# Linear attention, Fourier mixing and MLP on one core: attention of two batches in turns, and two plain MLP groups instead of four

## The chip, the cores and the metric

The kernel runs on one core of a Trainium2 chip. The metric is the device time of one execution in microseconds (us), a median over several runs. The run-to-run spread of one kernel is about 1%.

## The reference

Four batches of 768 rows go through a decaying linear attention with 8 heads of 64, and the result x (768 x 512 a batch) through a Fourier mixing block with an MLP:

```python
# attention, per block of 64 rows (cut)
intra = einsum('bhic,bhjc->bhij', qb, kb) * Dmask
out   = einsum('bhij,bhjd->bhid', intra, vb) + einsum('bhid,bhde->bhie', qb * lam_pow, kv_state)
kv_state = lam_block * kv_state + einsum('bhsd,bhse->bhde', kb * rev_pow, vb)

# mixing and MLP
X = fft(fft(x, axis=1), axis=2)
u = x + real(X)
un = (u - mean(u)) / sqrt(var(u) + 1e-06)
return u + maximum(un @ w_ch1, 0.0) @ w_ch2      # w_ch1 512 x 2048, w_ch2 2048 x 512
```

The two weights arrive with 64-bit elements and are decoded on the chip.

## The kernel before

All is fp32. A batch's attention has six chunks of 128 rows. Its transform folds x with its mirror image on VectorE, multiplies by tables on TensorE (`ys`), and then for three pairs of row tiles (t = 1, 2, 0) multiplies again, adds x, normalises and transposes into `ut`, the input of an MLP group. A group is two tiles of 128 rows; there are twelve. **Plain** groups are multiplied as they stand, from SBUF, while the front (attention, transforms) still runs. **Late** groups wait in device memory for the end, where two of them are done at a time with seven products instead of eight, which needs sums of weight blocks.

```python
    xp = plain_pool("xp", 2 * NC - 2)          # x tiles
    hp_ = plain_pool("hp", FO // 4 + 1)        # raw 64-bit weights, and hidden rows of plain groups
    pa = psums.enter_context(tc.tile_pool(name="pa", bufs=5, space=PS))
    pm = psums.enter_context(tc.tile_pool(name="pm", bufs=3, space=PS))
    # ... cut
    ORDER = [(b, g) for b in range(B) for g in (1, 2, 0)]
    PLAIN, LATE = ORDER[:4], ORDER[4:]
    # ... cut: the order, as generators whose pieces are woven
    run(weave(attn(0), part(w, 0.5 * NW), 0.5 * NW / t_att))
    fr, mix = chain(front(b) for b in range(1, B)), fft_ln(0)     # front = attention, then transform
    # ... cut: transform 0 woven with attention 1 and weights
    back = chain(mlp(b, g) for b, g in PLAIN)
    run(weave(part(fr, 2 * t_chunk), weave(part(back, FO * 1.7 - 1.0), w, 0.9), 1.5))
    run(w)
    run(weave(fr, back, (len(PLAIN) * t_mlp - FO * 1.7 - 25.0) / t_rest))
    # ... cut
    run(weave(combine_weights(0), back, 1.5))
    # ... cut
    run(combine_weights(1))
    for j in range(len(LATE) // 2):
        late(j)
```

A scheduler then orders each engine's instructions, mostly as the program has them, by what it takes to be ready and by free buffers. The program then fixes that order for each engine.

## Time and profile before

| kernel before | |
|---|---|
| time | 912.4 us (904.8 to 912.7) |
| span in the trace | 906.4 us, mean granted TensorE clock 0.975 of full speed |
| first late pair | at 513.1 us; four pairs of 96.7 us follow |
| TensorE busy ahead of it | 439.4 us, idle 73.6 us |

"Ahead of it" is what the change reorders: the rest is late pairs and some 7 us of end. The prediction shows the lines.

### The profile page before, as it was taken

Reading aid. Unit: us, or ns where it says so; the run is one execution under the profiler, and the core shown is the slowest. Engines: PE = TensorE matmul, PEld = TensorE weight load, DVE = VectorE, ACT = ScalarE, POOL = GpSimd, SP = SyncE. Lnnn points to the kernel's source line nnn. Section 1 sums busy time; section 2 is a strip of 40 time slices with the busy share of each in tenths; the row PEclk is TensorE's granted clock in tenths of the full one; section 3 lists DMA queues with packets and bytes.
Section 4 is the critical chain, followed back from the end, with each engine's and each line's share of the span. In section 5 each row is a group of like instructions: output and inputs, shape, how many; then the busy total and the mean of one; then the engine's idle time right before and its main releaser. Section 6 shows DMA issues by size and latency. Waiting matters only on the chain.

```text
span 906.4 us, 11761 instructions
## 1 busy us (share of the span) xinstructions
PE 826.5 (91%) x4660; PEld 652.9 (72%) x4660; DVE 437.0 (48%) x1006; ACT 209.0 (23%) x467; POOL 90.7 (10%) x108
## 2 busy tenths in 40 slices
PE   4775678699999999999999899999999999999997
PEld 2564566545865578567874588888888888888886
DVE  4779869854532135443567756115531454135410
ACT  3665436620211212223221021002200120012100
POOL 2214211100010110012200100000000000000000
PEclk9988789899999999999999999999999999999999
DMA  9899316611013241344216001110011100110010
GB/s 230 232 249 252 111 52 179 209 39 35 24 47 93 74 120 47 116 141 129 88 47 215 29 1 47 46 35 12 1 59 47 35 1 1 47 47 1 0 35 24
DMA packets 96190, 72.43 MB, mean 80 GB/s; under 512 B 77536, under 2 KB 79080, under 8 KB 96136
## 3 DMA queue, kind: packets, MB, share of 16 engines
q1 hardware_dynamic: 90176, 57.51, 22.3%
q0 software_dynamic: 2496, 7.87, 2.7%
q10 hardware_dynamic: 3464, 6.30, 2.0%
q8 instruction: 37, 0.61, 0.3%
q14 instruction: 17, 0.14, 0.0%
HBM read 50.68 MB, written 20.99 MB: 79 GB/s over the span
## 4 chain that ended last, share of the span: by engine, by line
PE 51%; DVE 5%; issue 1%; DMA 1%; POOL 1%; ACT 0%; POOLq 0%; DVEq 0%; ACTq 0%
PE p L627 21%; PE p L674 21%; PE pm L545 1%; PE pm L559 1%; PE pa L440 1%; PE pa L486 1%; PE pa L290 1%; PE pa L322 1%; DVE stt L470 1%; DVE w1s L604 1%; DVE w2s L604 1%; PE pa L318 1%; POOL rs L475 0%; DVE x L512 0%; DVE x L513 0%
## 5 line engine op out<-in xcount | busy, mean ns | idle before, releaser
L545 PE MATMUL pm<-ut,w 128*128 128x256 f32 x512 | 124.2, 392 | 10.0 <-ACT hr L553 8.2
L559 PE MATMUL pm<-w,hr 128*128 128x512 f32 x256 | 120.6, 602 | 0.0
L545 PEld LDWEIGHTS pm<-ut,w 128*128 128x128 f32 x512 | 95.9, 194 | 26.3 <-ACT hr L553 8.9
L627 PE MATMUL p<-ur,w 128*128 128x256 f32 x384 | 95.1, 382 | 3.3 <-DVE ur L620 1.9
L627 PEld LDWEIGHTS p<-ur,w 128*128 128x128 f32 x384 | 73.3, 191 | 14.5 <-issue 2.3
L559 PEld LDWEIGHTS pm<-w,hr 128*128 128x128 f32 x256 | 44.8, 190 | 40.3 <-issue 38.8
L627 PE MATMUL p<-us,w1s 128*128 128x256 f32 x256 | 66.6, 383 | 0.0
L674 PE MATMUL p<-w,hs 128*128 128x256 f32 x256 | 58.0, 379 | 0.5 <-DVE y L695 0.5
L674 PE MATMUL p<-w2s,hs 128*128 128x256 f32 x256 | 57.9, 379 | 0.0
L674 PE MATMUL p<-w,ha 128*128 128x256 f32 x256 | 57.9, 379 | 0.0
L535 POOL DMA_INDIRECT out_dram<-y,ix x12 | 13.3, 1109 | 409.9 <-DVE y L698 370.9
L627 PEld LDWEIGHTS p<-us,w1s 128*128 128x128 f32 x256 | 49.2, 192 | 6.9
L674 PEld LDWEIGHTS p<-w,hs 128*128 128x128 f32 x256 | 48.5, 190 | 7.5 <-DVE y L695 0.9
L674 PEld LDWEIGHTS p<-w2s,hs 128*128 128x128 f32 x256 | 48.6, 190 | 6.6
L674 PEld LDWEIGHTS p<-w,ha 128*128 128x128 f32 x256 | 48.6, 190 | 6.6
L290 PEld LDWEIGHTS pa<-qT,kT 64*128 64x128 f32 x384 | 30.1, 193 | 25.9 <-ACT qT L279 14.4
L654 ACT COPY ha<-p 128x256 f32<-128x256 f32 x32 | 11.9, 372 | 155.6 <-PE p L627 155.5
L290 PE MATMUL pa<-qT,kT 64*128 64x128 f32 x384 | 36.2, 291 | 11.7 <-ACT qT L279 10.0
L294 DVE TENSOR_TENSOR sc<-pa,decay 128x512 f32<-128x512 f32 x48 | 31.8, 684 | 29.1 <-PE pa L290 26.3
L322 PE MATMUL pa<-sc,v 128*64 128x128 f32 x384 | 31.2, 290 | 9.8 <-DVE sc L294 9.8
L665 DVE TENSOR_TENSOR ha<-p,ha 128x256 f32<-128x256 f32 x32 | 13.6, 425 | 47.1 <-ACT ha L664 47.1
L322 PEld LDWEIGHTS pa<-sc,v 128*64 128x64 f32 x384 | 23.4, 143 | 17.5 <-DVE sc L294 13.4
(141 smaller groups left out, 1188.3 us busy)
## 6 DMA issues: line engine op xcount, KB each, us to landing
raw<-in_moe_w_ch_dram SPq DMA_DIRECT2D x32, 512.0 KB, 5.2
k<-in_k_dram SPq DMA_DIRECT2D x24, 256.0 KB, 3.8
q<-in_q_dram SPq DMA_DIRECT2D x24, 256.0 KB, 3.9
v<-in_v_dram SPq DMA_DIRECT2D x24, 256.0 KB, 3.2
ud<-x SPq DMA_DIRECT2D x16, 256.0 KB, 2.1
utd<-ut SPq DMA_DIRECT2D x8, 512.0 KB, 3.3
u<-ud SPq DMA_DIRECT2D x16, 256.0 KB, 2.6
ur<-utd SPq DMA_DIRECT2D x8, 512.0 KB, 5.6
```

Source lines behind the costliest of these rows:

```text
L290: mm(pss[hi][:, hp, :], lhsT=kT[HD[hi], hp, :], rhs=qT[HD[hi], hp, :], start=True, stop=True)
L294: nc.vector.tensor_tensor(t, pss[hi], decay[:, hi::2, :], op=ALU.mult)
L318: mm(po[HD[hi], hp, :], lhsT=s_old[HD[hi], hp, :], rhs=qs[HD[hi], hp, :], start=(hp == 0), stop=False, skip_group_check=True)
L322: mm(po[HD[hi], hp, :], lhsT=vt[:, 2 * hp + hi, :], rhs=sc[hi][:, hp, :], start=(c == 0 and hp == 0), stop=(hp == HP - 1), skip_group_chec ...
L535: nc.gpsimd.indirect_dma_start(out=out.rearrange("b s d -> (b s) d"), out_offset=row_of(2 + HC * (b + 1) + T - HC), in_=y[:, :], in_offset ...
L545: nc.tensor.matmul(ps, lhsT=w1[:, c, 128 * fc:128 * fc + 128], rhs=ut[:, c, :], start=(c == 0), stop=(c == KO - 1))
L559: nc.tensor.matmul(ps, lhsT=hr[fc // 4][:, fc % 4, 128 * i:128 * i + 128], rhs=w2[:, fc, :], start=(fc == 0), stop=(fc == FO - 1))
L604: V.tensor_tensor(o[:, i:i + n // 2], x[:, i:i + n // 2], y[:, i:i + n // 2], op=op)
L627: nc.tensor.matmul(ps, lhsT=s2.A[a][:, kt, 128 * i:128 * i + 128], rhs=U[b][:, kt, :], start=(first and kt == 0), stop=(kt == 1), skip_gro ...
L654: nc.scalar.copy(a11, two(X))
L665: V.tensor_tensor(a22, two(Z), a22, op=ADD)
L674: nc.tensor.matmul(ps, lhsT=h[a][:, s, i, :], rhs=s2.B[b][:, i, :], start=(first and i == 0), stop=(i == HF - 1), skip_group_check=True)
```

## The change

The intent: a late pair costs TensorE less than a plain pair, so two of the four plain groups become late. The filler that they were is to be replaced by the attention of two batches in turns. To make room in SBUF, x goes through device memory and comes back when a transform wants it, one x tile and one buffer of `hp` are given up, and work moves from VectorE to ScalarE and GpSimd. The core of the diff (cut: indices of the mirror rows, the two sets of states, the fetches of x):

```diff
-    xp = plain_pool("xp", 2 * NC - 2)
+    xp = plain_pool("xp", 2 * NC - 3)
-    hp_ = plain_pool("hp", FO // 4 + 1)
+    hp_ = plain_pool("hp", FO // 4)
-    pa = ... bufs=5     pm = ... bufs=3
+    pa = ... bufs=6     pm = ... bufs=2
-            qs = new(at, [128, HP, C], "qs")
+            qs = new(at, [128, HP, C], "qs", bufs=2)
+            nb = new(np_, [128, G], "nb")
+            nc.vector.scalar_tensor_tensor(nb, mv[:, :, 0], -1.0, rs, op0=ALU.mult, op1=ALU.mult)
-                    nc.vector.tensor_scalar(o, x, mv[:, i, 0:1], rs[:, i:i + 1], op0=ALU.subtract, op1=ALU.mult)
+                    nc.scalar.activation(o, x, AF.Identity, bias=nb[:, i:i + 1], scale=rs[:, i:i + 1])
-    PLAIN, LATE = ORDER[:4], ORDER[4:]
+    PLAIN, LATE = ORDER[:2], ORDER[2:]
-            if fc % 2: nc.vector.tensor_scalar(t, ps, 0.0, None, op0=ALU.max)
-            else:      nc.scalar.activation(t, ps, AF.Relu)
+            nc.scalar.activation(t, ps, AF.Relu)
+            eng = nc.gpsimd if part == 0 and n >= 3 else V        # combining: half on GpSimd
+    att = chain([turns([attn(0), attn(1)]), turns([attn(2), attn(3)])])
+    mix = [fft_ln(b) for b in range(B)]
+    back, back2 = (mlp(b, g) for b, g in PLAIN)
+    run(weave(part(att, 2 * t_att - 1.0), part(w, 0.6 * NW), 0.6 * NW / (2 * t_att)))
+    # cut: transform 0 with 4 chunks of attention 2 and 3 and the rest of the weights;
+    #      transform 1 with 3 chunks and back; the last chunks with back;
+    #      transforms 2 and 3 with back2, a few us between their steps and 0.3 of their pace within
```

More of the change, by code (lines that the diff above doesn't have):

```diff
@@ L59, in _consts @@
     p = np.arange(128)
-    ha, hb = S - 256, 128 * (S // 256) + 128
+    hb = S - 256
     rev = [S - 128 * t - p for t in range(S // 256)]
-    rows = [S // 2 - 128 - p, np.maximum(S // 2 - 256 - p, 0)]
-    rows += [r - hb for r in rev[:2]] + [r - 128 for r in rev[2:]]
+    rows = [S // 2 - p, S // 2 - 128 - p]
+    rows += [r - hb for r in rev[:2]] + rev[2:]
     for b in range(B):
@@ L132 @@
     psums = ctx.enter_context(ExitStack())
-    pa = psums.enter_context(tc.tile_pool(name="pa", bufs=5, space=PS))
-    pm = psums.enter_context(tc.tile_pool(name="pm", bufs=3, space=PS))
+    pa = psums.enter_context(tc.tile_pool(name="pa", bufs=6, space=PS))
+    pm = psums.enter_context(tc.tile_pool(name="pm", bufs=2, space=PS))
     cnt = [0]
@@ L193 @@
     nc.gpsimd.memset(mhalf, -0.5)
-    st = [const.tile([128, HP, D], F32, name=f"st{i}") for i in range(2)]
+    st = [[const.tile([128, HP, D], F32, name=f"st{j}{i}") for i in range(2)] for j in range(2)]
     cs = const.tile([128, 2, 2, 2, NK], F32, name="cs")
@@ L249, in weights @@
             yield 1.0
-    xs, xn_, xd = {}, {}, {}
+    xs, xd = {}, {}
     def pair(t, hp):
@@ L296, in attn_chunk @@
         yield 1.5
-        s_old, s_new = st[(c + 1) % 2], st[c % 2]
+        s_old, s_new = st[b % 2][(c + 1) % 2], st[b % 2][c % 2]
         if not last:
@@ L330, in attn_chunk @@
         px = px.rearrange("p h e -> p (h e)")
-        x = xn_[b, c] = new(xp, [C, DM], "x") if c < HC else new(xn, [C, DM], "xn")
+        x = new(xn, [C, DM], "xn")
         nc.scalar.copy(x[:, 0:HM], px[:, 0:HM])
@@ L334, in attn_chunk @@
         if c == 0:
-            xd[b] = (dram.tile([S - 256, DM], F32, name=f"xa{b}"), dram.tile([257, DM], F32, name=f"xb{b}"))
+            xd[b] = (dram.tile([S - 128, DM], F32, name=f"xa{b}"), dram.tile([257, DM], F32, name=f"xb{b}"))
             nc.scalar.dma_start(xd[b][1][256:257], x[0:1])
-        elif c < NC - 1:
-            nc.scalar.dma_start(xd[b][0][(c - 1) * C:c * C], x)
+        if c < NC - 1:
+            nc.scalar.dma_start(xd[b][0][rows], x)
         if c >= NC - 2:
             nc.scalar.dma_start(xd[b][1][(c - NC + 2) * C:(c - NC + 3) * C], x)
-        if c == NC - 2:
-            mirror_a(b)
-        elif c == NC - 1:
-            mirror_b(b)
+        if b == 0 and c == NC - 2:
+            fetch_a(b)
         yield 1.7
@@ L357 @@
     gather = nc.gpsimd.indirect_dma_start
-    eo, r1s = {}, {}
+    eo, r1s, x3s = {}, {}, {}
     def fold_x(b, a, n, i, lo, hi):
@@ L368, in fold_x, with fetch_a @@
         tt(o[0:n, i, 1:HM], o[0:n, i, 1:HM], o[0:n, i, HM:DM - 1], op=ALU.subtract)
-    def mirror_a(b):
+    def fetch_a(b):
         xa = xd[b][0]
@@ L377, in mirror_a @@
             gather(out=r1[a][0:n], out_offset=None, in_=xa[:, :], in_offset=row_of(a, n))
+            nc.sync.dma_start(eo[b][a][1][0:n, 1, 0:DM], xa[S // 2 + 128 * a:S // 2 + 128 * a + n])
         for t in range(2, HC):
@@ L380, in mirror_a, with fetch_b @@
             gather(out=u[:, :], out_offset=None, in_=xa[:, :], in_offset=row_of(2 + t))
-    def mirror_b(b):
+        for t in range(HC):
+            u = xs[b, t] = new(xp, [128, DM], "x")
+            nc.sync.dma_start(u, xa[128 * t:128 * t + 128])
+    def fetch_b(b):
         for t in range(2):
@@ L385, in mirror_b @@
             gather(out=u[:, :], out_offset=None, in_=xd[b][1][:, :], in_offset=row_of(2 + t))
-        for t in range(HC):
-            xs[b, t] = xn_.pop((b, t))
     def fold_a(b):
@@ L391, in fold_a @@
         for a, n in enumerate(BLK):
-            fold_x(b, a, n, 1, r1[a][0:n], xn_[b, HC + a][0:n])
+            fold_x(b, a, n, 1, r1[a][0:n], eo[b][a][1][0:n, 1, 0:DM])
+        x3s[b] = new(fp, [1, DM], "r1")
+        nc.sync.dma_start(x3s[b], xd[b][0][S // 2:S // 2 + 1])
     def fold_b(b):
@@ L427, in fft_ln @@
     def fft_ln(b):
-        yield 1.0
+        if b > 0:
+            fetch_a(b)
+        fetch_b(b)
+        yield 2.0
         fold_a(b)
@@ L481, in norm @@
                 for o, x in ((un[:, 0:HM], u[:, 0:HM]), (un[:, HM:DM], u[:, DM - 1:HM - 1:-1])):
-                    nc.vector.tensor_scalar(o, x, mv[:, i, 0:1], rs[:, i:i + 1],
-                                            op0=ALU.subtract, op1=ALU.mult)
+                    nc.scalar.activation(o, x, AF.Identity, bias=nb[:, i:i + 1], scale=rs[:, i:i + 1])
                 pt = psum_a([128, KO, 128])
@@ L517, in fft_ln @@
                 width(HC, ps, True)
-                x3 = xn_.pop((b, HC))
+                x3 = x3s.pop(b)
                 nc.vector.tensor_tensor(even_odd(v_[0:1, 0:HM]), halves(ps[0:1])[:, ::-1, 0:QM],
@@ L549, in mlp @@
             t = hr[-1][:, fc % 4, :]
-            if fc % 2:
-                nc.vector.tensor_scalar(t, ps, 0.0, None, op0=ALU.max)
-            else:
-                nc.scalar.activation(t, ps, AF.Relu)
+            nc.scalar.activation(t, ps, AF.Relu)
             yield 1.7
@@ L600, in combine_weights @@
             s2.B = dict(b11=b11, b21=b21, b22=b22, t1=wz[:, 0], t2=wz[:, 1], t4=wz[:, 2], t3=b12)
-        for o, x, y, op in todo:
+        for n, (o, x, y, op) in enumerate(todo):
+            eng = nc.gpsimd if part == 0 and n >= 3 else V
             n = o.shape[1]
             for i in range(0, n, n // 2):
-                V.tensor_tensor(o[:, i:i + n // 2], x[:, i:i + n // 2], y[:, i:i + n // 2], op=op)
+                eng.tensor_tensor(o[:, i:i + n // 2], x[:, i:i + n // 2], y[:, i:i + n // 2], op=op)
                 yield 1.3
@@ L707, in attn @@
             yield from attn_chunk(b, c)
-    def front(b):
-        yield from attn(b)
-        yield from fft_ln(b)
     def weave(lead, other, ratio):
@@ L739, in chain, with turns @@
             yield from g
+    def turns(gens):
+        gens = list(gens)
+        while gens:
+            for g in list(gens):
+                d = next(g, None)
+                if d is None:
+                    gens.remove(g)
+                else:
+                    yield d
     NW = KO * DFF // WP
@@ L743 @@
     t_chunk = 7.3
-    t_att, t_front = NC * t_chunk, NC * t_chunk + 10.0 + 7.0 + 5.7 + 3 * 2.4
-    t_mlp = FO * 1.7 + G * 4 * 3.4
-    run(weave(attn(0), part(w, 0.5 * NW), 0.5 * NW / t_att))
-    fr, mix = chain(front(b) for b in range(1, B)), fft_ln(0)
-    next(mix)
-    run(weave(part(fr, t_chunk), part(w, 0.1 * NW), 0.1 * NW / t_chunk))
-    next(mix)
-    run(weave(part(fr, t_chunk), part(w, 0.1 * NW), 0.1 * NW / t_chunk))
-    next(mix)
-    run(part(fr, 0.5 * t_chunk))
-    run(weave(mix, weave(part(fr, 1.5 * t_chunk), part(w, 0.3 * NW), 0.3 * NW / 11.0), 0.5))
-    back = chain(mlp(b, g) for b, g in PLAIN)
-    run(weave(part(fr, 2 * t_chunk), weave(part(back, FO * 1.7 - 1.0), w, 0.9), 1.5))
-    run(w)
-    t_rest = 3 * t_front - 6 * t_chunk
-    run(weave(fr, back, (len(PLAIN) * t_mlp - FO * 1.7 - 25.0) / t_rest))
+    t_att = NC * t_chunk
+    att = chain([turns([attn(0), attn(1)]), turns([attn(2), attn(3)])])
+    mix = [fft_ln(b) for b in range(B)]
+    back, back2 = (mlp(b, g) for b, g in PLAIN)
+    run(weave(part(att, 2 * t_att - 1.0), part(w, 0.6 * NW), 0.6 * NW / (2 * t_att)))
+    next(mix[0])
+    run(weave(part(att, t_chunk), part(w, 0.1 * NW), 0.1 * NW / t_chunk))
+    next(mix[0])
+    run(part(att, t_chunk))
+    next(mix[0])
+    run(weave(part(att, t_chunk), part(w, 0.1 * NW), 0.1 * NW / t_chunk))
+    run(weave(mix[0], weave(part(att, t_chunk), part(w, 0.2 * NW), 0.2 * NW / t_chunk), 0.3))
+    next(mix[1])
+    ahead = weave(part(att, 3 * t_chunk), weave(part(back, FO * 1.7 - 1.0), w, 0.9), 1.3)
+    run(part(ahead, 10.0))
+    next(mix[1])
+    run(part(ahead, 10.0))
+    next(mix[1])
+    run(part(ahead, 10.0))
+    run(weave(mix[1], ahead, 1.5))
+    run(ahead)
+    run(w)
+    run(weave(att, back, 0.8))
+    run(back)
+    for b, n in ((2, 4.0), (3, 8.0)):
+        next(mix[b])
+        run(part(back2, n))
+        next(mix[b])
+        run(part(back2, n))
+        next(mix[b])
+        run(part(back2, 0.5 * n))
+        run(weave(mix[b], back2, 0.3))
     front_end.close()
@@ L766 @@
     load_u(0)
-    run(weave(combine_weights(0), back, 1.5))
-    run(back)
+    run(weave(combine_weights(0), back2, 1.0))
+    run(back2)
     plain_end.close()
```

## The prediction

> **What bounds the kernel now.** I read the page first, then busy time by stage, then the chain that ended last, then the waits of TensorE, then the costs of single operations. The page gives PE 91% of the span, which hides that the program has stages with different limits. I cut the span where the chain of waits changes its character (187 us: the first plain group's second product starts; 513 us: the first seven-product group starts) and asked for busy time in these three stretches:
>
> ```profile
> core 0: us, PE busy (x) PEld busy (x) DVE busy (x) ACT busy (x) POOL busy (x), PEclk, DMA share, GB/s
> 0.00:187.00 187.00, 126.38 (x1079) 101.52 (x1080) 144.85 (x298) 98.75 (x186) 43.02 (x49) 0.90 0.68 187
> 187.00:513.00 326.00, 312.99 (x1799) 211.47 (x1797) 149.36 (x321) 62.53 (x155) 39.98 (x51) 0.99 0.28 84
> 513.00:906.40 393.40, 387.15 (x1784) 339.87 (x1784) 142.81 (x390) 47.69 (x127) 7.68 (x8) 0.99 0.08 26
> ```
>
> Stage 1 (attention of batches 0 and 1, transform of batch 0, the weights decoded from 64 bits) has TensorE busy 68%, VectorE 77%, DMA 68%: nothing is full, so it is bound by chains between engines and by VectorE. Stage 2 (the other attention and transforms, with plain MLP groups as filler) is TensorE's: 313 of 326 us. Stage 3 (the late groups, seven products for eight) is all TensorE. Idle TensorE time is 187.0 - 126.4 = 60.6 us, 13.0 us and 6.2 us.
>
> The chain shows what a late pair of groups costs: the same piece starts every 96.7 us.
>
> ```profile
> 513.14 46.73 PE p L627 x208
> ...
> 610.80 45.76 PE p L627 x212
> ...
> 707.49 45.76 PE p L627 x212
> ...
> 804.19 45.76 PE p L627 x212
> ```
>
> A plain pair costs more. The groups of instructions have both products of all four plain groups:
>
> ```profile
> L545 PE MATMUL pm<-ut,w 128*128 128x256 f32 x512 | 124.2, 392 | 10.0 <-ACT hr L553 8.2
> L559 PE MATMUL pm<-w,hr 128*128 128x512 f32 x256 | 120.6, 602 | 0.0
> ```
>
> (124.2 + 120.6) / 4 = 61.2 us of busy TensorE for a group, 122.4 us for a pair.
>
> The waits of TensorE in stage 1 have no single culprit:
>
> ```profile
> PE pa L290 <- ACT qT L279: 10.0, 10, 2.1
> PE pa L322 <- DVE sc L294: 9.8, 9, 4.7
> PE pa L486 <- DVE un L482: 8.8, 5, 5.8
> PE pm L545 <- ACT hr L553: 8.2, 2, 6.1
> PE pa L329 <- ACT oT L325: 6.3, 8, 1.6
> ```
>
> Each is a chain of one attention batch, or of one normalisation, with nothing else ready. The attention of a second batch is what could stand there.
>
> **What the Trainium skill says.** "Perfetto Trace Analysis", section Identifying the Most-Contended Engine: matmul busy is a poor measure of nearness to the limit, weight-load busy a better one. The trace agrees: PE reads 96% in stage 2 and 98% in stage 3, weight loads 65% and 86%. Stage 2 looks full but is less dense, partly because its second product has 512 columns for each weight load. The same page, section Optimization Strategy: a kernel with several regimes may gain from interleaving them. That is the intent here; the 60.6 us idle of stage 1 are the room for it. "ScalarE: Activation LUTs", section What ACT_TABLE_LOAD costs: each per-partition pointer operand adds about 93 ns to an ACTIVATE. The kernel before has no two-pointer ACTIVATE, so the trace does not show it; its plain 128x256 copy takes 372 ns. "GPSIMD Engine Reference", section 3.1: a two-input fp32 operation on GpSimd takes about twice VectorE's time (1.96). The trace agrees roughly: 128x512 takes 1118 ns there and 684 ns on VectorE, a ratio of 1.6.
>
> **The change part by part.**
>
> (a) Two plain groups become one more late pair. TensorE loses 122.4 us of busy time in stages 1 and 2, and stage 3 gains 96.7 us. This is the only certain gain: 25.7 us, if idle time stays as it is. But some of the busy figure is overlap and lower clock: where matmuls run in a row, the chain shows 1.73 us for 8 of the first product and 0.86 us for 2 of the second, so a plain group is 128 x 0.216 + 64 x 0.43 = 55.2 us and a pair 110.4. Against that the gain is 13.7 us. The rest of the 25.7 comes only if what is left runs no less densely.
>
> (b) The removed groups were the filler of stage 2. What has to be there instead is attention in turns. In stage 1 the new order puts 16 chunks (12 of batches 0 and 1, 4 of batches 2 and 3) with all weights and the transform of batch 0, and hardly any MLP. Before, it held 12 chunks and about 32 us of MLP. TensorE busy: 126.4 - 32.4 + 4 x 6 = 118 us (6 us: L272 to L329 busy over 24 chunks). Is another engine the bound? VectorE: 144.9 us, plus 4 chunks at 2.5 us (two scores at 0.68, one scaled q at 0.69, one state at 0.41), less 4.4 us of normalisation and some 6 us of relu: about 145 us. With two independent attentions I take it at 83% busy instead of 77%: 175 us. DMA: 0.68 busy over 187 us at most, plus 4 x 0.79 MB of q, k, v and about 2 MB more x traffic: about 140 us of time, not the bound over all. So stage 1 takes about 175 us, with 57 us idle on TensorE.
>
> (c) What is left for stage 2: 439.4 - 122.4 - 118 = 199 us of busy TensorE, with 8 chunks, three transforms and nearly two plain groups. A transform is the weak place, as its chain for each pair of tiles shows (batch 3, second of three):
>
> ```profile
> 475.44 0.68 DVE x L512
> 476.12 0.60 DVE x L513
> 476.73 1.20 DVE stt L470 x2
> 477.92 0.23 DVE mv L471 x2
> 478.23 0.23 POOL ve L474
> 478.53 0.72 POOL rs L475
> 479.28 0.42 DVE un L482
> 479.83 0.67 PE pa L486 x4
> 480.50 0.86 PE pm L559 x2
> 481.37 0.44 PE pa L486 x4
> ```
>
> From one such chain to the next it is 8.9 us (466.08 to 475.44 to 484.33 is 9.4 and 8.9), with some 2.3 us of TensorE in it: 18 to 20 us of a transform's 27 need a filler. Before, a plain group was always at hand. Now the transforms of batches 2 and 3 share one group of 55 us, and need about 2 x 19 for their chains, 2 x 8 for the folds on VectorE ahead of their first products and a few us for combining weights: as much as there is, with no slack, and the share woven into the chains themselves is small (0.3). I estimate 17 us more idle than before here: 13 + 17 = 30 us, so stage 2 is 199 + 30 = 229 us.
>
> (d) Normalisation on ScalarE: 48 operations leave VectorE (17.6 us). On ScalarE I estimate 372 + 2 x 93 = 558 ns from the row and the skill's figure, so the chain of a pair grows by 4 x 0.15 us plus about 0.2 us for the new VectorE operation and its hop: 0.8 us, where no filler hides it. Counted in the 17 us of (c). Relu all on ScalarE is 32 operations as before, off the path.
>
> (e) x through device memory adds per batch a write and about four and a half reads of 256 KB, some 6 MB over the kernel, beside 72 MB. Its latency (the chain has 2.0 us for the write, 3.2 for the gather) is the one the gathers already have. Half of the combining goes to GpSimd: six operations of 1.2 us become about 2 us each, beside VectorE's six.
>
> The sum: 175 + 229 = 404 us to the first late pair (513 before), 5 x 96.7 = 483 us, and 6.5 us at the end as before: 894 us. That is 12 us less than the trace's 906.4. The new order was evidently adjusted piece by piece (ratios, portions), so I expect stage 1 or the fillers to come out somewhat better than my crude estimates: 5 us off, and 2 us from the span to the timed run (908.4 against 906.4). **889 to 891 us; I put 889.**
>
> **The rivals.**
>
> *Starved transforms.* With little filler, batches 2 and 3 run as bare chains: 2 x (27 + 10 + 8) = 90 us with only 28 + 55 us of dense TensorE beside, and batch 1's transform also waits for tile buffers held by the first plain group. For it: the buffers are nine where two transforms want twelve, and the one set of fold tiles keeps batches apart. Against: the two attentions in turns leave batch 2 ahead of batch 3. Then idle in stage 2 is 45 to 50 us and the time about 910: no gain.
>
> *Stage 1 much denser.* Two attentions give work at every wait listed above; if VectorE reaches 90%, stage 1 is about 160 us and the time 874. For it: the waits in stage 1 are many and short. Against: the DMA share is 0.91 in the first 64 us, so doubling attention there meets the memory.
>
> *ScalarE as the new bound.* 98.8 us busy in stage 1 plus about 4 chunks of 2.4 and 7 us of normalisation is 115 of 175: no bound by itself, but its order may delay copies. I give it 5 us at most.
>
> **Range and chances.** The fixed terms (late pair, end) are known to 1 or 2 us; stage 1 to about 12, the idle of stage 2 to about 12. Together some 17 us: 870 to 908. Two per cent below a before of about 909 is 891, just above my middle: faster 0.52, same 0.41, slower 0.07.
>
> **What would show it.** Right: five late pieces 96.7 us apart; the first at about 400 us; weights decoded by 170 to 180 us; VectorE over 80% until then; TensorE idle about 30 us from there to the first late pair, mostly at the transforms of batches 2 and 3 under waits for the normalisation, ACTIVATEs of about 0.56 us. Wrong: a first late pair before 385 us (stage 1 denser) or after 415 us (starved transforms), or late pairs that are not 96.7 us.

## The result

The changed kernel takes 973.7 us (969.5 to 983.3) against 912.4, a ratio of 1.071 with a 95% interval of 1.061 to 1.081. Here and below a ratio is the mean time of one kernel's runs over that of the other's of the same rounds, so it is not quite the ratio of the medians. It is slower by 7%, where 889 us was forecast and "slower" was given a chance of 0.07.

The chain of waits of the kernel after has late pairs of the cost forecast. They just start much later:

```profile
483.01 48.13 PE p L631 x208
...
582.08 45.76 PE p L631 x212
...
678.77 45.76 PE p L631 x212
```

The pairs are 96.7 us apart from the second on, five of them and the end make 491.7 us, as predicted. But the first one starts at 483 us instead of 404. Nearly all of the miss lies ahead of it. The busy time by stage, cut where the weights are decoded and where the late stage begins:

```profile
core 0: us, PE busy (x) PEld busy (x) DVE busy (x) ACT busy (x) POOL busy (x), PEclk, DMA share, GB/s
0.00:260.00 260.00, 174.77 (x1553) 142.63 (x1554) 169.58 (x331) 123.87 (x241) 50.62 (x62) 0.84 0.66 176
260.00:483.00 223.00, 168.15 (x940) 112.87 (x940) 100.58 (x205) 60.51 (x147) 42.74 (x42) 0.88 0.32 105
```

The columns are the stretch, its length, and busy time of TensorE, its weight loads, VectorE, ScalarE and GpSimd; then the granted TensorE clock. TensorE is idle for 85 us in the first and 55 us in the second stretch, 140 us together, where I had expected 87. It is also busy for 342.9 us where 317 were expected: the matmuls are as many as before's less those of two plain groups (2878 - 384, within one), but the clock granted is 0.84 and 0.88, against 0.90 and 0.99 before. That the lower clock makes them longer fits, but no run shows it for the whole front. That splits the 79 us: 53 idle, 26 busy.

The end of the second stretch is the barest. First the kernel before, from the last product of batch 3's transform with the tables to the last transpose, and on to the first late pair:

```profile
463.50:491.50 28.00, 25.96 (x120) 17.12 (x120) 16.44 (x42) 5.62 (x17) 2.81 (x6) 1.00 0.38 136
491.50:513.00 21.50, 18.32 (x47) 8.35 (x45) 21.39 (x24) 0.96 (x2) 2.41 (x1) 1.00 0.32 118
```

The same two stretches of the kernel after:

```profile
426.50:463.30 36.80, 13.20 (x58) 9.83 (x57) 13.81 (x31) 10.84 (x28) 9.41 (x9) 0.61 0.34 128
463.30:483.00 19.70, 2.71 (x8) 1.85 (x8) 19.70 (x14) 0.95 (x2) 10.13 (x4) 0.59 0.19 67
```

Three normalisation chains and the combining of weights take 49.5 us before and 56.5 us after. The length differs by 7 us; what differs more is what TensorE does meanwhile. Before, it had 44 us of work in there, most of it plain MLP. After, it has 16. The timeline shows one bare chain of the kernel after (start, length, engine and line, operation, and in brackets the idle time before it and what ended that):

```profile
432.69 1.09 ACT L489 ACTIVATE un<-x,nb,rs 128x256 f32<-128x256 f32 x2 [4.92 <-issue]
433.35 1.18 PE L492 MATMUL pa<-ident,un 128*128 128x128 f32 x4 [6.11 <-ACT un L489]
...
444.40 1.09 ACT L489 ACTIVATE un<-x,nb,rs 128x256 f32<-128x256 f32 x2 [4.91 <-issue]
```

TensorE sits for 6.1 us until ScalarE's normalised tile comes, and the same step of the next pair comes 11.7 us later. Over the whole kernel this is now TensorE's longest wait; the list of waits has it at 40.0 us for 16 times, before it was 13.2 us:

```profile
PE pa L492 <- ACT un L489: 40.0, 16, 7.9
PE p L631 <- DVE us L622: 17.0, 1, 17.0
```

### The profile page after: what moved, and what is told of

The parts are those of the page before. It is cut to its first block, busy times and chain, and to the rows that moved or that the text cites. A ratio compares the mean times of both kernels' runs of the same rounds, so it can differ in the third digit from the quotient of the medians.

```text
span 974.7 us, 12084 instructions
## 1 busy us (share of the span) xinstructions
PE 828.2 (85%) x4724; PEld 681.9 (70%) x4724; DVE 449.1 (46%) x1022; ACT 244.0 (25%) x547; POOL 103.1 (11%) x114
## 4 chain that ended last, share of the span: by engine, by line
PE 50%; issue 3%; DVE 2%; DMA 0%; POOL 0%; ACT 0%; POOLq 0%; DVEq 0%
PE p L631 25%; PE p L678 24%; DVE w1s L608 1%; DVE w L608 0%; DMA out_dram<-y,ix 0%; PE pa L492 0%; POOL rs L480 0%; ACT un L489 0%; DVE stt L475 0%; POOLq L828 0%; DVE x L518 0%; DVE us L622 0%; DVE us L621 0%; DVE x L519 0%; POOL ve L479 0%
## 5 line engine op out<-in xcount | busy, mean ns | idle before, releaser
L631 PE MATMUL p<-ur,w 128*128 128x256 f32 x480 | 119.7, 385 | 0.0
L631 PEld LDWEIGHTS p<-ur,w 128*128 128x128 f32 x480 | 93.1, 194 | 13.1
L631 PE MATMUL p<-us,w1s 128*128 128x256 f32 x320 | 84.0, 386 | 17.0 <-DVE us L622 17.0
L551 PE MATMUL pm<-ut,w 128*128 128x256 f32 x256 | 64.8, 406 | 9.9 <-ACT hr L556 9.8
L678 PE MATMUL p<-w,hs 128*128 128x256 f32 x320 | 72.4, 380 | 0.5 <-DVE y L699 0.5
L551 PEld LDWEIGHTS pm<-ut,w 128*128 128x128 f32 x256 | 50.6, 205 | 18.5 <-ACT hr L556 11.2
L562 PE MATMUL pm<-w,hr 128*128 128x512 f32 x128 | 58.0, 596 | 0.0
L492 PE MATMUL pa<-ident,un 128*128 128x128 f32 x96 | 23.3, 353 | 40.3 <-ACT un L489 40.0
L631 PE MATMUL p<-us,w 128*128 128x256 f32 x160 | 41.1, 379 | 0.0
L631 PE MATMUL p<-ur,w1s 128*128 128x256 f32 x160 | 41.1, 379 | 0.0
```

Of the source, the lines that this page charges most:

```text
L492: nc.tensor.transpose(pt[:, c, :], un[:, 128 * c:128 * c + 128], ident)
L551: nc.tensor.matmul(ps, lhsT=w1[:, c, 128 * fc:128 * fc + 128], rhs=ut[:, c, :], start=(c == 0), stop=(c == KO - 1))
L562: nc.tensor.matmul(ps, lhsT=hr[fc // 4][:, fc % 4, 128 * i:128 * i + 128], rhs=w2[:, fc, :], start=(fc == 0), stop=(fc == FO - 1))
L631: nc.tensor.matmul(ps, lhsT=s2.A[a][:, kt, 128 * i:128 * i + 128], rhs=U[b][:, kt, :], start=(first and kt == 0), stop=(kt == 1), skip_gro ...
L678: nc.tensor.matmul(ps, lhsT=h[a][:, s, i, :], rhs=s2.B[b][:, i, :], start=(first and i == 0), stop=(i == HF - 1), skip_group_check=True)
```

## The experiments

The main theory, **A**, is that the two plain groups were the filler of the front and that nothing took their place. The rivals: **B**, the new order is to blame (B1: the turns, in in-order queues); **C**, the moves between engines; **W**, the late weights; **K**, the low clock. The interval of the kernel after is itself wide, 1.061 to 1.081, so a single gain of under some 10 us is not settled by the time alone; where one is given, it comes from medians. In the diffs, "before" and "after" name the kernel that was edited.

### Two plain groups alone (b_plain2)

```diff
 (before)
-    PLAIN, LATE = ORDER[:4], ORDER[4:]
+    PLAIN, LATE = ORDER[:2], ORDER[2:]
```

> The kernel before with one line changed: two plain groups instead of four, everything else (order, pools, engines) as before. Theory A (the filler is what was lost: without two plain groups the transforms run as bare chains, and the rest of the change does not make up for it): the saving of about 26 us on TensorE is eaten, 905 to 940 us, no faster than before. Theory B (the new order of attention, weights and transforms is to blame, fewer plain groups are harmless): 885 to 897 us, faster than before by about 2%.

Measured: 940.3 us, ratio 1.035 (1.027 to 1.043). Theory A holds at the upper edge of its range, B's number is far off. The late stage starts at 447.2 us, only 66 us earlier, though about 110 us of TensorE's work left the front. The stages of this run, to compare with 187 and 326 us before:

```profile
0.00:187.00 187.00, 125.64 (x1064) 100.87 (x1064) 144.22 (x297) 97.28 (x183) 45.12 (x51) 0.89 0.70 192
187.00:447.00 260.00, 205.07 (x1428) 145.99 (x1428) 139.33 (x298) 57.60 (x142) 34.56 (x47) 0.89 0.35 106
```

The first stage is unchanged. In the second, idle time grew from 13 to 55 us and the clock fell from 0.99 to 0.89. TensorE's wait for normalised tiles grew from 13.2 to 31.0 us. So this one line makes about half of the slowdown.

### Attention one batch after the other (a_turns)

```diff
 (after)
-    att = chain([turns([attn(0), attn(1)]), turns([attn(2), attn(3)])])
+    att = chain([attn(b) for b in range(B)])
```

> The kernel after with the attentions one after the other again, all else as after. Theory B1 (attention in turns blocks the in-order queues: chunks of two batches wait in TensorE's and in the DMA queue's order, and the weights behind them): faster than after by 15 us or more, weights decoded before 230 us instead of 255. Theory A: within 10 us of the 974 of after, or slower, as single chains have less to stand beside them.

Measured: 982.5 us, ratio 1.078 (1.070 to 1.086), and the late stage starts at 491.4 us instead of 483.0. B1 falls: the turns are not the fault. They seem worth some 8 us, but the two intervals overlap.

### Three moves between engines undone (a_undo_eng), and each of them

```diff
 (after)
-                    nc.scalar.activation(o, x, AF.Identity, bias=nb[:, i:i + 1], scale=rs[:, i:i + 1])   # and nb
+                    nc.vector.tensor_scalar(o, x, mv[:, i, 0:1], rs[:, i:i + 1], op0=ALU.subtract, op1=ALU.mult)
-            nc.scalar.activation(t, ps, AF.Relu)
+            if fc % 2: nc.vector.tensor_scalar(t, ps, 0.0, None, op0=ALU.max)
+            else:      nc.scalar.activation(t, ps, AF.Relu)
-            eng = nc.gpsimd if part == 0 and n >= 3 else V
+            eng = V
```

> The kernel after with three moves between engines undone together: normalisation on VectorE, half of relu on VectorE, all combining of weights on VectorE. Theory C (the longer norm chain[...] cost the time): 974 goes to 940 or below. Theory A or B (order and filler): 955 to 972, some 8 us from twelve shorter norm chains and 5 us from the combining at the end.

Measured: 960.3 us, ratio 1.054 (1.047 to 1.061), late stage from 467.9 us: 14 us gained. That is inside what A and B foresaw and not the 940 of theory C (whose other half, that GpSimd and VectorE slow each other, a_comb tests). The normalisation alone (a_norm, the first edit above):

> The kernel after with only the normalisation back on VectorE (relu and combining as in after). By the traces the ScalarE form adds 2 x 0.19 us for each tile, with 0.2 us for the new VectorE operation: 12 pairs of tiles at 0.8 to 1.3 us, most of them exposed. If that is what the undoing of all three moves gained: 961 to 966 us. If it was relu's: 970 to 976 us.

Measured: 968.5 us, ratio 1.066 (1.062 to 1.071), some 4 to 5 us. The combining alone (a_comb, the last edit):

> The kernel after with all combining of weights on VectorE. In the trace of after six combining operations on VectorE took 13 us beside GpSimd's (1.2 us each before), and the late stage began 20 us after the last transpose. All twelve on VectorE should take 12 x 1.2 = 14.5 us, and no operation is held up by GpSimd: start of the late stage 4 to 6 us earlier, 967 to 971 us. If the two engines did not slow each other, it would be 3 us later.

Measured: 974.9 us, ratio 1.070 (1.062 to 1.077), late stage from 483.9 us: nothing. The mutual slowing of the two engines is there, as the timeline of the kernel after shows:

```profile
456.70 2.29 DVE L482 SCALAR_TENSOR_TENSOR nb<-mv,rs 128x2 f32<-128x2 f32 x1 [1.13 <-POOL rs L480]
461.23 12.20 POOL L608 TENSOR_TENSOR w2s<-w,w2s 128x1024 f32<-128x1024 f32 x4
463.30 4.66 DVE L608 TENSOR_TENSOR w1s<-w 128x1024 f32<-128x1024 f32 x2 [4.31 <-PE pa L492]
467.88 6.63 DVE L608 TENSOR_TENSOR w1s<-w1s,w 128x1024 f32<-128x1024 f32 x2
```

Beside GpSimd, VectorE takes 3.3 us (last row) for an operation that takes 1.21 alone; GpSimd takes 3.3 beside VectorE and 2.35 with VectorE idle. The first row is a tiny operation of the last normalisation, which takes 0.16 us elsewhere: GpSimd's combining had just begun. In a_comb that chain is 2.1 us shorter, which the spread of the times hides. After the last transpose nothing is gained: combining takes 18.2 us on VectorE alone and 18.0 us shared. Relu alone (a_relu, the second edit):

> The kernel after with half of relu back on VectorE, nothing else. By difference it should hold most of what the three engine moves gained (ratio 1.071 to 1.054, of which the normalisation gave 0.5 points and the combining nothing): ratio 1.058 to 1.064, 963 to 968 us, and the wait of TensorE's first plain product for relu (9.9 us in after) mostly gone. Rival (relu is off the path, the three moves gain only together): ratio 1.068 to 1.073.

Measured: 973.0 us, ratio 1.071 (1.063 to 1.078): nothing, against my expectation; TensorE's wait for relu is 8.4 us against 9.8. So of 14 us that the three gain together, one gains 5 alone and the other two nothing. One part of what joins them is in the trace of a_norm: the last normalisation, now on VectorE, runs beside GpSimd's combining.

```profile
444.85 4.69 POOL L607 TENSOR_TENSOR w2s<-w 128x1024 f32<-128x1024 f32 x2
444.92 4.76 DVE L487 TENSOR_SCALAR un<-x,mv,rs 128x256 f32<-128x256 f32 x2 [1.14 <-POOL rs L480]
```

Its operations take up to 2.42 us instead of 0.41, and from `rs` to the late stage's first sum it is 25.1 us, against 21.6 in a_undo_eng. That is 3.5 us of the 8 to 9 missing. The rest stays open; relu and combining were not run in pairs with the normalisation.

### The fifth buffer of raw weights and hidden rows (a_hr5)

```diff
 (after)
-    hp_ = plain_pool("hp", FO // 4)
+    hp_ = plain_pool("hp", FO // 4 + 1)
```

> The kernel after with the fifth buffer of the pool that holds both raw weights and hidden rows given back. Theory W1 (with four buffers the plain group's four hidden tiles leave the last raw weights one buffer, so that load and decode take turns, 6.5 us a piece from 231 to 255 us): weights decoded by about 235 us, late stage 12 to 20 us earlier, 955 to 962 us. Rival (the weights are late because the one in-order DMA queue holds them behind q, k and v of chunks that TensorE has not reached): under 5 us, 969 to 975 us.

Measured: 964.1 us, ratio 1.059 (1.052 to 1.066); the last weight's ScalarE step starts at 239.5 us instead of 252.0, and the late stage at 471.2 instead of 483.0. W1 is right, a little smaller than I put it: 964.1 us is just above its range. TensorE's waits for relu fall from 9.8 to 2.7 us. The rows behind it, from the timeline of the kernel after, show the seven last weight loads spread over 30 us and TensorE waiting for relu:

```profile
217.97 30.52 SPq L227 DMA_DIRECT2D raw<-in_moe_w_ch_dram  x7
...
255.26 6.24 PE L551 MATMUL pm<-ut,w 128*128 128x256 f32 x16 [7.27 <-ACT hr L556]
```

A plain group holds four such buffers for its hidden rows. With four in all, the loads get what the group has not yet taken, and the group's last hidden tile waits until the weights give one up.

### All weights early (a_wearly)

```diff
 (after)
-    run(weave(part(att, 2 * t_att - 1.0), part(w, 0.6 * NW), 0.6 * NW / (2 * t_att)))
+    run(weave(part(att, 2 * t_att - 1.0), part(w, 0.9 * NW), 0.9 * NW / (2 * t_att)))
+    run(w)
```

> The kernel after with all weights woven into the attention of batches 0 and 1 (0.9 of them instead of 0.6, the rest at once after). Theory W (late weights hold back the first plain group and with it everything after): weights decoded before 200 us, late stage 15 to 40 us earlier, 935 to 960 us. Rival (the first stage is bound by VectorE and memory whatever the order, so that the attention gets later by what the weights get earlier): 965 to 980 us.

Measured: 975.1 us, ratio 1.073 (1.067 to 1.079). The last weight's ScalarE step starts at 153 us instead of 252, but the fourteenth chunk of attention ends at 167 us instead of 130 and the first transform's products at 200 us instead of 160. The late stage starts at 480.4 us instead of 483.0. So the rival was right: in the first stage, one kind of work comes later by what another comes earlier.

### The tenth x tile (a_xp10)

```diff
 (after)
-    xp = plain_pool("xp", 2 * NC - 3)
+    xp = plain_pool("xp", 2 * NC - 2)
```

> The kernel after with ten x tiles instead of nine. Two batches' six and four held by plain groups are ten, so with nine the transform of batch 1 waits for the first plain group's result. Theory X (that wait holds the second stage back): late stage 5 to 15 us earlier, 960 to 970 us. Rival (TensorE is busy with that plain group anyway, so it costs nothing): within 4 us of 974.

Measured: 964.7 us, ratio 1.061 (1.056 to 1.065), late stage from 473.0 us. Batch 1's transform has its products with the tables from 222 to 250 us instead of 224 to 292. In the kernel after, 30 of these 40 come only from 287 us on, after a plain group's first result at 280.5 us has freed an x tile; in a_xp10 they don't wait for it. Theory X holds.

### The PSUM banks as before (a_psum)

```diff
 (after)
-    pa ... bufs=6     pm ... bufs=2
+    pa ... bufs=5     pm ... bufs=3
```

> The kernel after with the PSUM banks shared out as before, five to attention and transforms, three to the MLP. If two banks for the MLP were a cost of their own (TensorE must wait for each relu): ratio under 1.066. If the sixth bank helps the two attentions: above 1.075. I expect neither: 1.067 to 1.074.

Measured: 974.6 us, ratio 1.073 (1.068 to 1.079). As expected, no effect.

### The small losses together (a_fix, a_all3)

a_fix is a_hr5 and a_undo_eng in one kernel.

> The kernel after with the fifth buffer for raw weights and hidden rows and with the three moves between engines undone (the two runs that each gained, 10 and 14 us, together). If they are separate costs: 974 - 10 - 14 = 950 us, 945 to 955. If they are one cost seen twice (both only shorten the wait for the first plain group): 957 to 962 us. In either case not near the kernel before: the order itself, with bare transforms at the end, keeps the rest.

Measured: 950.4 us, ratio 1.045 (1.041 to 1.049): they add up. a_all3 has a_xp10 too, and `qs` with one buffer for the room.

> The kernel after with everything undone that gained alone: the fifth buffer (10 us), the three moves between engines (14), the tenth x tile (9; one scaled-q buffer is given up for the room). If these small losses add up, 974 - 33 = 941 us, 935 to 947, which would be the time of the kernel before with two plain groups and nothing else changed (940), so that the rest of the change (order, turns, x through memory) nets to nothing. If they overlap, 947 to 955 us, and the order has a cost of its own.

Measured: 938.7 us, ratio 1.031 (1.027 to 1.035), late stage from 450.9 us. This is the time of b_plain2. So the 33 us between b_plain2 and the kernel after are accounted for by the hidden-row buffer, the engine moves and the x tile. What stays of the change, the turns, the order and x through device memory, comes to nothing in sum. That is a sum: if the turns alone are a gain, something in the rest costs about as much.

### Four plain groups in the new order (a_plain4)

```diff
 (after)
-    PLAIN, LATE = ORDER[:2], ORDER[2:]
+    PLAIN, LATE = ORDER[:4], ORDER[4:]
-    back, back2 = (mlp(b, g) for b, g in PLAIN)
+    back, back2 = mlp(*PLAIN[0]), chain(mlp(b, g) for b, g in PLAIN[1:])
```

> The kernel after with four plain groups again, the three last of them beside the transforms of batches 2 and 3. Theory A (filler): TensorE is no longer idle in the last transforms; late stage starts at about 483 + 110 - 45 = 545 us, and with one late pair less the time is 920 to 945 us. Theory B (order): the first stage is as slow as in after and nothing is regained at the end: 950 us or more.

Measured: 963.2 us, ratio 1.057 (1.051 to 1.063), late stage from 568.1 us. Filler returned without the lost buffers helps by only 10 us, which is B's number. It tells that A alone is not the whole: this order with these buffers delays the first plain group whatever follows (its second product starts at 258 us here, at 261 in the kernel after, at 187 in the one before). It does not tell order and buffers apart.

### Matmuls to keep the clock up (a_warm)

```diff
 (after, ahead of each normalisation's transposes)
+            if b == 3:
+                hot = psum_m([128, DM])
+                for _ in range(10):
+                    nc.tensor.matmul(hot, lhsT=ident, rhs=w2[:, 0, :], start=True, stop=True)
```

> The kernel after with ten matmuls whose result nobody reads put ahead of each normalisation of batch 3, where TensorE waits about 6 us for it. In after these chains ran at a granted clock of 0.59 and took 11.7 us each, against 8.9 in the kernel before at 1.00. Theory K (the low clock lengthens the chains by some 1.4 us each): clock above 0.8 there, chains 10.2 to 10.8 us, 968 to 972 us. Rival (the chain is engine hops, the clock is nothing): chains still 11.7 us or longer for the extra work, 974 to 980 us.

Measured: 975.9 us, ratio 1.072 (1.066 to 1.077). The stretch by stretch view shows that it did to the clock what it should:

```profile
427.00:463.00 36.00, 33.49 (x130) 18.79 (x130) 14.50 (x35) 10.44 (x26) 5.44 (x8) 1.00 0.27 96
```

The clock was 1.00 instead of 0.61, and from one normalisation to the next it was 10.9 us (439.09 to 450.00) instead of 11.7. So the clock is worth 0.8 us a chain, about half of what I gave it, and the total shows nothing of it. Two or three times 0.8 us are below the spread, and batch 3's transform was 5 us late in the profiled run before any added matmul. The low clock is mostly a companion of the idle time in these chains. It was tried in batch 3 alone; that the longer busy time elsewhere costs something is not excluded.

### Attention as the filler, in the old kernel (b_over2, b_over4)

```diff
 (before; b_over4 is this alone, b_over2 has two plain groups as well)
-    fr, mix = chain(front(b) for b in range(1, B)), fft_ln(0)
+    def fronts():
+        yield from attn(1)
+        for b in range(1, B):
+            nxt = attn(b + 1) if b + 1 < B else iter(())
+            yield from weave(fft_ln(b), nxt, 1.3)
+            yield from nxt
+
+    fr, mix = fronts(), fft_ln(0)
```

> The kernel before with two plain groups, and each batch's transform woven with the next batch's attention (before: attention and transform of a batch follow each other, with MLP as the only filler). Theory A says that the 940 us of the two-group run come from transforms without a filler; attention can stand in for it in batches 1 and 2, some 15 us each: 905 to 925 us. If the transforms' chains are limited by something that attention shares (VectorE, the in-order queues): 930 to 945 us.

Measured: 901.5 us, ratio 0.991 (0.983 to 0.998), 39 us less than b_plain2 and a little better than expected. Its second stage, to be held against b_plain2's above:

```profile
187.00:409.50 222.50, 195.36 (x1362) 136.60 (x1361) 143.41 (x300) 55.37 (x138) 42.19 (x46) 0.97 0.40 120
```

Nearly the same work with 27 us idle instead of 55, at a clock of 0.97 instead of 0.89. The late stage starts at 409.5 us. TensorE's wait for normalised tiles is 14.3 us instead of 31.0. This is the strongest test of theory A: one edit of the order, which gives the transforms a filler, separates it from b_plain2. The woven order also leaves plain MLP for batch 3's transform, which had none in the kernel after, nor in b_plain2: TensorE is busy for 26.7 of the 28.5 us of its three chains.

> The kernel before with four plain groups and the transforms woven with the next batch's attention, as in the 901 us run but without the fewer plain groups. Theory A: with four groups TensorE was already 96% busy in the second stage (13 us idle), so better order has little to find: 903 to 912 us, and the gain of the 901 us run needs both, fewer plain groups and another filler. Rival (the gain is the order's alone, fewer plain groups give nothing): 895 to 902 us.

Measured: 905.3 us, ratio 0.996 (0.991 to 1.001). As expected, with four plain groups the new filler has little left to fill. So it isn't the order as such that gains 39 us, but the order where a filler is missing. Fewer plain groups lose 30 us without it; with it they are 4 us better, about half a per cent between ratios whose intervals overlap.

### Off the path: sums of the second weights (b_defer2, b_defer2r)

b_defer2 is b_over2 with the sums of `w_ch2` blocks moved into the first late loop, one half operation an iteration:

```diff
 (b_over2; cut: the rest of s2.rest after the loop, and where it is made)
-            todo = [(ws[:, 0], ...), (ws[:, 1], ...), (ws[:, 2], ...), (wz[:, 0], ...), (wz[:, 1], ...), (wz[:, 2], ...)]
+            todo = [(ws[:, 0], ...), (ws[:, 1], ...), (ws[:, 2], ...)]
-            todo = [(a21, a11, a21, SUB), (b12, b22, b12, SUB)]
+            if part == 2: todo = [(wz[:, 0], ...), (wz[:, 1], ...), (wz[:, 2], ...), (b12, b22, b12, SUB)]
+            else:         todo = [(a21, a11, a21, SUB)]
             last = (i, X, Z)
+            if j == 0:
+                next(s2.rest, None)
```

> The 901 us kernel (two plain groups, transforms woven with the next batch's attention) with the sums of the second weights, which no product needs in the first 47 us of the late stage, moved from ahead of that stage into its first loop. TensorE was idle for 6.9 us before its first product with summed weights, with VectorE busy on 8 x 1.2 us of such sums. Expected: late stage starts 6 to 9 us earlier, 892 to 896 us, 1.5 to 2% faster than before. If VectorE then holds up the late loop (it is some 60% busy there) the gain is under 3 us.

Measured over six runs: 897.8 us (892.0 to 901.7), ratio 0.986 (0.981 to 0.991). The gain over b_over2 is about 4 us where 6 to 9 were expected, and the two intervals overlap. TensorE's 6.9 us wait is gone, but waits for VectorE appear in the loop (1.36 us at 415 us is the first). This is the best version: faster than both kernels, though not by 2%. b_defer2r differs in one number, 0.9 for 1.3 in the weave:

> As the last, with attention woven into the transforms at 0.9 instead of 1.3 of their pace, so that more of it is left for after a transform. If the balance of attention and transforms matters now: 5 us or more off the last run's time, in either direction. If TensorE is near enough full in that stage: within 4 us of it.

Measured: 902.1 us, ratio 0.992 (0.987 to 0.997), 4 us worse on the same chip. The balance matters a little; this is not settled to better than that.

## Why the prediction was wrong

- **The late pair (a) was right.** 96.7 us each, five of them and the end 491.7 us in the trace; predicted 489.5 (483 and 6.5).
- **Step (b) failed: stage 1 in 175 us, VectorE at 83%.** Its sixteen chunks were done in time, at 161 us, but batch 0's last transpose came at 197 us (144 before), as the order puts twelve chunks ahead of that transform (done at 110 us) and no longer six (64 us), and the weights at 255; VectorE was busy for 61% of the first 175 us and 65% of the first 260. TensorE idled for 85 us where I put 57. (By 260 us two more chunks and a plain group's first product were done too, so stage 2 had less left.) I took two attentions for enough work at every wait. By a_turns they help by some 8 us. a_wearly shows that attention, transform and weights only push each other about. And I read the fewer `hp` buffers in the diff without costing them: a_hr5 puts 10 us on that line.
- **Step (c) failed in size: 30 us of idle in stage 2.** It was 55. The mechanism was named: transforms need some 19 us of filler each and there was no slack. But I spread the one plain group evenly over two transforms, and the trace has its last product end at 415 us, before batch 3's chains began. Two terms were missing: the x tile (9 us, a_xp10; I had named the wait for it only under a rival) and the longer busy time, 342.9 us instead of 317.
- **The rival of starved transforms was right in kind and too small.** I gave it 910 us. Two plain groups without another filler, all else as before, are 940.
- **Step (d) was right for the operation and too small for the chain.** The two-pointer ACTIVATE takes 594 ns where I estimated 558. But batch 3's first bare chain, to the next one, takes 11.7 us with it and 10.3 with the normalisation on VectorE (a_norm, a_undo_eng): 1.4 us, not 0.8. Of the 2.7 us more than before's 9.0, that and the clock's 0.8 leave 0.5 open. a_norm gave back only 4 to 5 us in all.
- **Step (e)** put GpSimd's combining at about 2 us an operation; it took 2.35 alone and 3.3 beside VectorE, and slowed VectorE's. The prediction's ratio of 1.6 set a GpSimd operation on SBUF beside one of VectorE that reads PSUM; on operands of the same shape in SBUF it is 2.35 to 1.21, or 1.9. a_comb shows that the combining cost nothing that the times show.
- **The sum was of single terms each taken at its best.** The range added the errors of the two stages as if they were independent; idle time was over by 28 and by 25 us, both upwards. I then took 5 us off because the order looked tuned. The trace of before spoke against it: 13 us idle in stage 2 meant that filler was exactly used, not that it was plenty.
- The intent itself was sound. b_over2 starts its late stage at 409.5 us, close to my 404, with the same plain and late groups. That the two numbers are so near is partly luck, as its order is not the one that I costed. It reaches that by giving each transform a filler, and without any of the changes to buffers and engines.

## What to carry to other kernels

Work that fills the waits of a latency-bound stage costs less there than its time on the engine: here some 110 us of it were taken out, and the front got 66 us shorter. Before moving it, list each chain that it hides, its length and its engine's share, and name what will stand there instead, chain by chain. And cost every buffer that a diff takes away, above all one that two kinds of tiles share.

## What the Trainium skill lacked or had wrong

- "TensorE: Matmul & The Clock Gate", Part 1, has the clock at half after an idle window. The traces agree as far as they show it: their clock records are 0.5 or 1.0, with a mean of 0.59 to 0.61 where TensorE was busy for about a third or less, and 1.00 when a_warm filled the gaps. The page doesn't tell what that is worth in a chain bound by other engines: here 0.8 of 11.7 us, and nothing in the total.
- No page that I used warns that tiles of two kinds (raw weights and hidden rows) that share one set of buffers hold each other up: one buffer of five was worth 10 us.
